# The four operand sums of a fast matrix product, moved from VectorE to GpSimd

## Chip, core and metric

The kernel runs on one core of one Trainium2 chip. The metric is the device time of one execution in microseconds. Its engines are TensorE (PE in the profile; PEld is its weight load), VectorE (DVE), ScalarE (ACT), GpSimd (POOL) and SyncE (SP, which issues most of the DMAs).

## What is computed

Retention (attention with a decay instead of a softmax) over 4 batches, 8 heads, 576 tokens and head size 64, and behind it two feed-forward layers of 2304 tokens, 512 features and 2048 hidden features, all in float32:

```python
scores = scale * np.matmul(q, k.transpose(0, 1, 3, 2))
ret = scores * Dmat[None, :, :, :]            # gamma_h ** (i - j) for i >= j, else 0
x = np.matmul(ret, v)                         # -> 2304 x 512
h = x @ moe_w_in;  x = np.maximum(0.01 * h, h) @ moe_w_out
h = np.maximum(x @ moe2_w_in, 0.0);  out = (h * h) @ moe2_w_out
```

## The kernel before, in words

**Numbers.** A float32 operand of a feed-forward product is kept as two rounded halves, `hi` (a ScalarE copy that rounds) and `lo` (a VectorE subtraction of the rest), and a product is three matmuls: hi x hi, hi x lo, lo x hi.

**The first product** of a layer is done by a Strassen-like scheme: data and weights are cut into four blocks, and seven products of sums and differences of blocks take the place of eight. The tokens are cut into three parts of 768 (`p` = 0 to 2), and the 2048 hidden features into four groups (`g`). For each layer, group and part, `first` does the seven products into the PSUM tiles `a` and `b`, in the order 0 to 6, and `second` multiplies the result by the output weights into PSUM tiles `yps`, in two halves of tokens (t = 0, 1). The sums over groups are kept in `ysb[p]`: for the first group ScalarE copies them (line 428), for later ones VectorE adds them (line 430).

**The operands of the data** are made once for each layer and part, by the generator `operands(layer, p)`: six builds in all. Of the blocks b11, b21, b12, b22 of `ysb[p]` it makes b11, b21, t2 = b22 - (b12 - b11), b22 - b12, b12 - b11, b21 - t2 and b22, in place, with the four subtractions of lines 270, 272, 275 and 281, each 128 x 768 elements. For each of the seven it writes a `hi` (line 256, ScalarE) and a `lo` (line 260, VectorE) into an `x` tile. These tiles are stored to DRAM (line 237) and loaded again for the later groups (line 304).

**When.** The builds are written out between other work by hand-set tables and a pace: `operands(0, 0)` runs in steps during the attention part (the first 87 us or so), and `operands(layer, p + 1)` during the second product of part p of group 0; `operands(1, 0)` during that of the last part of the last group of layer 0. In the same places stand the steps of the weights (`steps_in`, lines 149 to 187, and `steps_out`, lines 199 to 216), which unpack, sum and split the weights on ScalarE and VectorE. Each engine then works its own list in the order in which it was written. So one VectorE list holds the builds, the weights' steps, the sums `t` of the first product (lines 370, 384, 389), its activation (line 329), its `glo` (line 356), the output sums (line 430), and in the attention part the masked scores (line 515).

**GpSimd** has, before, only the decays of the attention part: line 524 scales q, line 528 scales k, in place, one pair for each chunk of tokens; there are 20 chunks (0 to 19), the last of each five half as long.

Waits that matter below: line 370 adds the second product (in `b`) and the ScalarE copy `s` of the first, and the fourth product can't be written into `b` before it has read; the seventh, into `a`, waits in the same way for line 384; and a `yps` group of the second half of tokens waits until the bank of the first half is read (line 428 or 430).

Of the kernel before, what the change touches and what calls it, by code (L numbers as in the profile page):

```python
# [50 lines left out]
def retention_ffn_kernel(ctx: ExitStack, tc: tile.TileContext, full, rows, half, halfv, w1, w2, const, mask, gk, out):  # L51
# [12 lines left out]
    nc = tc.nc  # L64
    sub, mul, add, mx = ALU.subtract, ALU.mult, ALU.add, ALU.max
# [23 lines left out]
    def f32(ap):  # L89
        return ap.bitcast(F32)  # L90
# [151 lines left out]
    def operands(layer, p):  # L242

        x = ysb[p].rearrange("p (k t n) -> p k t n", k=NK, t=2)
        b11, b21, b12, b22 = (x[:, k : k + 2, t] for t in range(2) for k in (0, 2))
        t2 = stage.tile([P, 2, HT], F32, tag="t2", name="t2")

        xt = {}

        def hi(i, src):  # L250
            use = layer, 0, p, i
            while uses[loaded[0]] != use or loaded[0] == used[0] + SLOTS:
                yield True
            loaded[0] += 1
            xt[i] = xs[use] = xpool.tile([P, 2, 2, HT], F32R, tag="x", name="x")
            nc.scalar.activation(xt[i][:, 0], src, AF.Copy)

        def lo(i, src):
            t = xt[i]
            nc.vector.tensor_tensor(t[:, 1], src, f32(t[:, 0]), sub)  # L260
            kept.append(((layer, 0, p, i), t))


        yield from hi(0, b11)
        yield
        yield from hi(1, b21)
        lo(0, b11)
        yield
        lo(1, b21)
        nc.vector.tensor_tensor(b11, b12, b11, sub)  # L270
        yield
        nc.vector.tensor_tensor(t2, b22, b11, sub)
        yield
        yield from hi(2, t2)
        nc.vector.tensor_tensor(b12, b22, b12, sub)
        yield
        yield from hi(3, b12)
        lo(2, t2)
        yield
        yield from hi(4, b11)  # L280
        nc.vector.tensor_tensor(b21, b21, t2, sub)
        yield
        yield from hi(5, b21)
        lo(3, b12)
        yield
        yield from hi(6, b22)
        lo(4, b11)
        yield
        lo(5, b21)
        yield  # L290
        lo(6, b22)
        yield
# [296 lines left out]
    with tc.manual_schedule():  # L589
        with tc.tile_pool(name="att", bufs=1) as pool:  # L590
# [22 lines left out]
            for i in range(n):  # L613
# [16 lines left out]
                if a < 2 * HT <= a + t:  # L630
                    builds.append(operands(0, 0))
# [26 lines left out]
        for layer in range(2):  # L658
            for g in range(NG):
# [25 lines left out]
                for p in range(NB):  # L685
                    built = [15 * p + 8]
                    if g == 0 and p + 1 < NB:
                        builds.append(operands(layer, p + 1))
                    elif layer == 0 and g == NG - 1 and p == NB - 1:
                        builds.append(operands(1, 0))  # L690

                    def in_first(m):
                        if i == p == m == 0:
                            return
                        pace(15 * p + m + 1, max(start, limit - 3))

                    def in_second(t, j, part):

                        if t or j or part in (0.5, 1):
                            pace(15 * p + 7 + 4 * t + 2 * (j + part), limit if p == NB - 1 else max(start, limit - 3))  # L700
                        load_x()

                    gs = first(layer, g, p, in_first)
                    second(layer, g, p, gs, in_second)
                    build(99)
# [58 lines left out]
```

## Time and profile before

| | us |
|---|---|
| median of 3 runs | 840.95 |
| lowest and highest run | 840.44 and 841.79 |
| span of the profiled execution | 840.4 |
| TensorE busy | 824.5 (98%) |
| VectorE busy | 601.4 (72%), 734 instructions |
| ScalarE busy | 340.2 (40%) |
| GpSimd busy | 44.3 (5%), 36 instructions, all in the first 77 us |

The span runs from the first to the last instruction; the page gives no other time of the profiled execution. It agrees with the lowest run. An engine's list is read by its rows: start, duration, line, and in brackets the idle time before it with what ended that. The reported duration of a VectorE or GpSimd instruction begins when it is issued, so time in which it was held is in it.

### The profile page before, as it was taken

Reading aid. Unit: us, or ns where it says so; the run is one execution under the profiler, and the core shown is the slowest. Engines: PE = TensorE matmul, PEld = TensorE weight load, DVE = VectorE, ACT = ScalarE, POOL = GpSimd, SP = SyncE. Lnnn points to the kernel's source line nnn. Section 1 sums busy time; section 2 is a strip of 40 time slices with the busy share of each in tenths; the row PEclk is TensorE's granted clock in tenths of the full one; section 3 lists DMA queues with packets and bytes.
Section 4 is the critical chain, followed back from the end, with each engine's and each line's share of the span. In section 5 each row is a group of like instructions: output and inputs, shape, how many; then the busy total and the mean of one; then the engine's idle time right before and its main releaser. Section 6 shows DMA issues by size and latency. Waiting matters only on the chain.

```text
span 840.4 us, 12382 instructions
## 1 busy us (share of the span) xinstructions
PE 824.5 (98%) x5084; PEld 776.9 (92%) x5084; DVE 601.4 (72%) x734; ACT 340.2 (40%) x447; POOL 44.3 (5%) x36
## 2 busy tenths in 40 slices
PE   7999999999999999999999999999999999999998
PEld 6888899999999999999999998998998998998996
DVE  4698789657666566658668879868777778754534
ACT  1454667544523433434425365543322333321211
POOL 3755000000000000000000000000000000000000
PEclk8999999999999999999999999999999999999999
DMA  9898463967646637746823554966855655735811
GB/s 349 330 322 292 170 258 114 420 250 260 247 180 250 248 135 292 259 140 233 307 101 122 191 226 163 385 246 233 296 178 203 263 182 231 263 140 199 288 51 75
DMA packets 45688, 191.01 MB, mean 227 GB/s; under 512 B 5696, under 2 KB 6720, under 8 KB 45632
## 3 DMA queue, kind: packets, MB, share of 16 engines
q1 hardware_dynamic: 45200, 189.44, 60.7%
q8 instruction: 40, 0.66, 0.3%
q10 hardware_dynamic: 432, 0.79, 0.3%
q14 instruction: 16, 0.13, 0.0%
HBM read 152.45 MB, written 37.75 MB: 226 GB/s over the span
## 4 chain that ended last, share of the span: by engine, by line
PE 84%; DVE 9%; ACT 3%; DMA 2%; issue 2%; SPq 0%; DVEq 0%; ACTq 0%
PE yps L419 44%; PE a L318 21%; PE b L318 15%; DMA raw<-in_w 1%; DVE r L515 1%; PE ops L544 1%; ACT sf L149 1%; PE ops L541 1%; DMA ysb<-in_w 1%; DVE x L260 1%; PE scps L513 1%; DVE sf L163 1%; DVE ilo L187 1%; PE sums L550 1%; DVE sf L205 1%
## 5 line engine op out<-in xcount | busy, mean ns | idle before, releaser
L318 PE MATMUL a<-x,ihi 128*128 128x384 f32 x768 | 196.1, 336 | 2.7 <-DVE t L384 2.4
L318 PE MATMUL b<-x,ihi 128*128 128x384 f32 x576 | 146.6, 335 | 0.8 <-DVE t L370 0.8
L318 PEld LDWEIGHTS a<-x,ihi 128*128 128x128 f32 x768 | 138.5, 188 | 5.8 <-DVE t L384 4.0
L419 PE MATMUL yps<-ghi,ohi 128*128 128x384 f32 x384 | 128.6, 335 | 0.6 <-ACT ysb L428 0.6
L318 PE MATMUL a<-x,ilo 128*128 128x384 f32 x384 | 128.5, 335 | 0.0
L419 PE MATMUL yps<-ghi,olo 128*128 128x384 f32 x384 | 128.3, 334 | 0.0
L419 PE MATMUL yps<-glo,ohi 128*128 128x384 f32 x384 | 128.3, 334 | 0.0
L356 DVE TENSOR_TENSOR glo<-t,ghi 128x768 fp32r<-128x768 f32 x96 | 91.7, 955 | 46.1 <-ACT ghi L351 45.6
L430 DVE TENSOR_TENSOR ysb<-yps,ysb 128x384 f32<-128x384 f32 (+1 forms) x126 | 76.0, 610 | 62.5 <-PE yps L419 62.1
L419 PE MATMUL yps<-ohi,glo 128*128 128x512 f32 x288 | 112.3, 390 | 0.0
L419 PE MATMUL yps<-olo,ghi 128*128 128x512 f32 x288 | 112.3, 390 | 0.0
L419 PE MATMUL yps<-ohi,ghi 128*128 128x512 f32 x288 | 112.1, 389 | 0.0
L351 ACT ACTIVATE ghi<-t 128x768 fp32r<-128x768 f32 x96 | 81.1, 845 | 68.5 <-DVE t L329 55.1
L318 PEld LDWEIGHTS b<-x,ihi 128*128 128x128 f32 x576 | 103.8, 188 | 1.7 <-DVE t L370 1.1
L344 ACT ACTIVATE s<-a 128x768 f32<-128x768 f32 x47 | 38.2, 814 | 156.2 <-PE a L318 156.1
L318 PE MATMUL b<-x,ilo 128*128 128x384 f32 x288 | 96.3, 334 | 0.0
L419 PEld LDWEIGHTS yps<-ghi,ohi 128*128 128x128 f32 x384 | 72.1, 188 | 1.6 <-ACT ysb L428 0.9
L318 PEld LDWEIGHTS a<-x,ilo 128*128 128x128 f32 x384 | 72.1, 188 | 0.0
L419 PEld LDWEIGHTS yps<-glo,ohi 128*128 128x128 f32 x384 | 72.1, 188 | 0.0
L419 PEld LDWEIGHTS yps<-ghi,olo 128*128 128x128 f32 x384 | 72.1, 188 | 0.0
L419 PEld LDWEIGHTS yps<-ohi,glo 128*128 128x128 f32 x288 | 54.0, 188 | 11.3
L419 PEld LDWEIGHTS yps<-olo,ghi 128*128 128x128 f32 x288 | 54.1, 188 | 11.0
(67 smaller groups left out, 997.3 us busy)
## 6 DMA issues: line engine op xcount, KB each, us to landing
x<-x SPq DMA_DIRECT2D x168, 768.0 KB, 5.9
raw<-in_w SPq DMA_DIRECT2D x62, 512.0 KB, 5.0
kv<-in_rows SPq DMA_DIRECT2D x16, 512.0 KB, 5.8
out<-ysb SPq DMA_DIRECT2D x18, 256.0 KB, 2.0
q<-in_full SPq DMA_DIRECT2D x16, 256.0 KB, 4.5
kt<-in_full SPq DMA_DIRECT2D x13, 256.0 KB, 4.7
ysb<-in_w SPq DMA_DIRECT2D x2, 512.0 KB, 6.8
kt<-in_full ACTq DMA_DIRECT2D x3, 256.0 KB, 5.6
```

The lines of the kernel that those rows point to most:

```text
L149: nc.scalar.activation(f32(a), f32(raw[:, :, 1]), AF.Abs)
L163: nc.vector.scalar_tensor_tensor(a, high, 1 << 31, a, ALU.bitwise_and, ALU.bitwise_or)
L187: nc.vector.tensor_tensor(lo[:, a:z], sf[:, a + 1 : z + 1], f32(hi[:, a:z]), sub)
L205: nc.vector.scalar_tensor_tensor(rest, high, 23, low, ALU.logical_shift_left, ALU.bitwise_or)
L260: nc.vector.tensor_tensor(t[:, 1], src, f32(t[:, 0]), sub)
L318: nc.tensor.matmul(ps[:, u, :HT], a[:, w, s], x[:, b, k], start=(start and k == 0 and i == 0), stop=(k == 1 and i == 2), skip_group_check= ...
L344: nc.scalar.activation(t, ps[:, :, :HT], AF.Copy)
L351: nc.scalar.activation(h, t, AF.Copy)
L356: nc.vector.tensor_tensor(l, t, f32(gs[key][0]), sub)
L419: nc.tensor.matmul(acc, a, b, start=(j == u == i == 0), stop=(j == 1 and u == NU - 1 and i == 2))
L430: nc.vector.tensor_tensor(y, acc, y, add)
L513: nc.tensor.matmul(ps[:n, j, p, :n], k[s, c], q[s, c], start=True, stop=True)
```

## The change

The four subtractions are issued on GpSimd; the operands, the places where they are written, and everything else stay.

```diff
@@ -267,18 +267,18 @@
         lo(0, b11)
         yield
         lo(1, b21)
-        nc.vector.tensor_tensor(b11, b12, b11, sub)
-        yield
-        nc.vector.tensor_tensor(t2, b22, b11, sub)
+        nc.gpsimd.tensor_tensor(b11, b12, b11, sub)
+        yield
+        nc.gpsimd.tensor_tensor(t2, b22, b11, sub)
         yield
         yield from hi(2, t2)
-        nc.vector.tensor_tensor(b12, b22, b12, sub)
+        nc.gpsimd.tensor_tensor(b12, b22, b12, sub)
         yield
         yield from hi(3, b12)
         lo(2, t2)
         yield
         yield from hi(4, b11)
-        nc.vector.tensor_tensor(b21, b21, t2, sub)
+        nc.gpsimd.tensor_tensor(b21, b21, t2, sub)
         yield
         yield from hi(5, b21)
         lo(3, b12)
```

GpSimd's list in the attention part, `operands(0, 0)` (`ysb_66` is `ysb[0]`, `t_557` its `t2`):

```order
+L270 TENSOR_TENSOR ysb_66<-ysb_66 128x2x384
 L528 TENSOR_TENSOR kv<-kv,gk 128x512
 L524 TENSOR_TENSOR q<-q,gq_77 128x512
 L528 TENSOR_TENSOR kv<-kv,gk 128x512
+L272 TENSOR_TENSOR t_557<-ysb_66 128x768
 L524 TENSOR_TENSOR q<-q,gq_78 128x512
 L528 TENSOR_TENSOR kv<-kv,gk 128x512
 L524 TENSOR_TENSOR q<-q,gq_79 128x512
 L528 TENSOR_TENSOR kv<-kv,gk 128x512
+L275 TENSOR_TENSOR ysb_66<-ysb_66 128x2x384
 L524 TENSOR_TENSOR q<-q,gq_80 128x256
+L281 TENSOR_TENSOR ysb_66<-ysb_66,t_557 128x2x384
```

The four subtractions stand between the decays of chunks 14 to 19; the other twenty follow on GpSimd behind the last decay, with nothing between them.

VectorE's list in the second product of layer 0, group 0, part 0, where `operands(0, 1)` is built (`ysb_67` is `ysb[1]`, `t_1164` its `t2`, `sf` and `raw` belong to the weights' steps):

```order
 L260 TENSOR_TENSOR x<-ysb_67,x 128x768
-L270 TENSOR_TENSOR ysb_67<-ysb_67 128x2x384
-L161 TENSOR_SCALAR sf<-sf 128x1024
-L163 SCALAR_TENSOR_TENSOR sf<-raw,sf 128x1024
-L272 TENSOR_TENSOR t_1164<-ysb_67 128x768
-L165 TENSOR_SCALAR sf<-sf 128x1024
-L168 SCALAR_TENSOR_TENSOR sf<-raw,sf 128x1024
-L275 TENSOR_TENSOR ysb_67<-ysb_67 128x2x384
+L161 TENSOR_SCALAR sf<-sf 128x1024
+L163 SCALAR_TENSOR_TENSOR sf<-raw,sf 128x1024
+L165 TENSOR_SCALAR sf<-sf 128x1024
+L168 SCALAR_TENSOR_TENSOR sf<-raw,sf 128x1024
```

The weights' steps close up; only the subtractions left the list.

VectorE's list in the second product of the last group and part of layer 0, where `operands(1, 0)` is built and the output sums of `ysb[2]` (`ysb_68`) are VectorE's:

```order
 L260 TENSOR_TENSOR x<-ysb_66,x 128x768
-L270 TENSOR_TENSOR ysb_66<-ysb_66 128x2x384
-L187 TENSOR_TENSOR ilo<-sf,ihi 128x1024
-L430 TENSOR_TENSOR ysb_68<-yps,ysb_68 128x384
-L272 TENSOR_TENSOR t_4206<-ysb_66 128x768
-L430 TENSOR_TENSOR ysb_68<-yps,ysb_68 128x384 x2
-L275 TENSOR_TENSOR ysb_66<-ysb_66 128x2x384
+L187 TENSOR_TENSOR ilo<-sf,ihi 128x1024
+L430 TENSOR_TENSOR ysb_68<-yps,ysb_68 128x384 x3
 L260 TENSOR_TENSOR x<-t_4206,x 128x768
```

The second to fourth output sums of the first half of tokens now follow each other behind line 187.

The waits of the moved instructions on GpSimd: line 270 waits for the `lo` of b11 (line 260, the first of a build) and, in the first build, its `hi`; line 272 for line 270; line 275 for nothing further; line 281 for the `lo` of b21 (the second) and for line 272. ScalarE's `hi` of t2, b12 and b21 wait for lines 272, 275 and 281.

## Rows read from the trace of the kernel before

**Rows 1.** The page, part 4: the chain that ended last, by engine.

```profile
PE 84%; DVE 9%; ACT 3%; DMA 2%; issue 2%; SPq 0%; DVEq 0%; ACTq 0%
```

**Rows 2.** Busy time by stretch: window, length, busy us and (instructions) of each engine.

```profile
104.00:124.00 20.00, 20.00 (x118) 19.94 (x117) 18.29 (x23) 11.87 (x20) 0.00 (x0) 1.00 0.61 236
449.00:457.00 8.00, 7.98 (x46) 7.39 (x44) 7.62 (x11) 3.26 (x5) 0.00 (x0) 1.00 0.48 197
515.00:533.00 18.00, 18.00 (x90) 15.95 (x89) 17.20 (x20) 10.92 (x16) 0.00 (x0) 1.00 0.70 268
```

**Rows 3.** Waits: who for whom, us in total, times, longest us.

```profile
PE a L318 <- DVE t L384: 2.4, 3, 1.1
...
PEld yps L419 <- DVE ysb L430: 0.6, 2, 0.3
```

**Rows 4.** VectorE's groups by line and form: xcount, busy us, mean ns.

```profile
L275 DVE TENSOR_TENSOR ysb<-ysb 128x768 f32<-128x768 f32 x6 | 5.7, 948 | 0.0
```

**Rows 5.** Timeline of GpSimd, 37 to 45 us: start, duration, instruction.

```profile
37.46 1.04 POOL L528 TENSOR_TENSOR kv<-kv,gk 128x512 f32<-128x512 f32 x1
38.47 1.26 POOL L524 TENSOR_TENSOR q<-q,gq 128x512 f32<-128x512 f32 x1
...
41.14 0.73 POOL L524 TENSOR_TENSOR q<-q,gq 128x256 f32<-128x256 f32 x1
```

**Rows 6.** Timeline of all engines, 65 to 78 us, in the attention part.

```profile
68.01 1.21 DVE L515 TENSOR_TENSOR r<-scps,mask 128x1024 f32<-128x1024 f32 x1
...
68.95 1.26 POOL L524 TENSOR_TENSOR q<-q,gq 128x512 f32<-128x512 f32 x1
...
69.15 2.15 DVE L209 SCALAR_TENSOR_TENSOR sf<-raw,sf 128x1024 uint32<-128x1024 uint32 x1
...
70.19 2.02 POOL L528 TENSOR_TENSOR kv<-kv,gk 128x512 f32<-128x512 f32 x1
...
71.23 1.79 DVE L272 TENSOR_TENSOR t<-ysb 128x768 f32<-128x768 f32 x1
...
73.21 1.13 PE L544 MATMUL ops<-q,state 128*128 128x128 f32 x8 [1.36 <-ACT state L556]
...
77.61 0.69 PE L550 MATMUL sums<-kv 128*64 128x64 f32 x16
```

**Rows 7.** Timeline of VectorE and TensorE, 104 to 123 us, build 2.

```profile
104.78 0.95 DVE L260 TENSOR_TENSOR x<-ysb,x 128x768 fp32r<-128x768 f32 x1
...
106.41 0.69 DVE L159 TENSOR_SCALAR sf<-sf 128x1024 f32<-128x1024 f32 x1 [0.67 <-ACT sf L149]
...
115.96 3.56 DVE L260 TENSOR_TENSOR x<-ysb,x 128x768 fp32r<-128x768 f32 x4
...
121.48 0.95 DVE L370 TENSOR_TENSOR t<-b,s 128x768 f32<-128x768 f32 x1
...
122.58 0.53 PE L318 MATMUL b<-x,ihi 128*128 128x384 f32 x2
```

**Rows 8.** Timeline of VectorE: line 370 of the part after builds 3 and 5.

```profile
153.99 0.96 DVE L370 TENSOR_TENSOR t<-b,s 128x768 f32<-128x768 f32 x1 [2.98 <-PE b L318]
...
498.69 0.96 DVE L370 TENSOR_TENSOR t<-b,s 128x768 f32<-128x768 f32 x1 [3.44 <-PE b L318]
```

**Rows 9.** Timeline of VectorE and TensorE, 449 to 458 us, build 4.

```profile
450.79 0.96 DVE L187 TENSOR_TENSOR ilo<-sf,ihi 128x768 fp32r<-128x768 f32 x1 [0.38 <-ACT ihi L185]
...
455.00 0.55 DVE L430 TENSOR_TENSOR ysb<-yps,ysb 128x384 f32<-128x384 f32 x1
...
455.61 0.19 PEld L419 LDWEIGHTS yps<-ghi,ohi 128*128 128x128 f32 x1 [0.27 <-DVE ysb L430]
```

**Rows 10.** Timeline of VectorE and TensorE, 515 to 533 us, build 6.

```profile
516.47 0.95 DVE L260 TENSOR_TENSOR x<-ysb,x 128x768 fp32r<-128x768 f32 x1
...
531.14 0.96 DVE L370 TENSOR_TENSOR t<-b,s 128x768 f32<-128x768 f32 x1
...
532.95 0.51 PE L318 MATMUL b<-x,ihi 128*128 128x384 f32 x2
```

## The prediction

> **What bounds the kernel now.** I read the chain of waits first. By engine it gives PE 84% and DVE 9% [rows 1], so the span is TensorE's, and VectorE matters only where the chain passes through it. The busy time by stretch shows where that can be [rows 2]: in three stretches that hold builds of the first product's operands, VectorE is busy 18.29 of 20, 7.62 of 8 and 17.20 of 18 us; a fourth lies in the attention part. The list of waits then shows what TensorE waits for: 2.4 us for `t` of line 384, and its weight loads 0.6 us for the `ysb` sums of line 430 [rows 3]. So the margins between VectorE and TensorE are small in these stretches, and what the change does to VectorE there decides; in the rest of the run VectorE has slack and the moved lines don't occur.
>
> **What it removes.** There are 24 instructions: lines 270, 272, 275 and 281, six of each. One takes 0.95 us on VectorE [rows 4]; in a row of such instructions the starts lie 0.87 us apart (four in 3.56 us) [rows 7], so a build sheds 4 x 0.87 = 3.5 us of VectorE.
>
> **What it adds.** GpSimd has no such instruction before. Its nearest rows are products of two SBUF tiles [rows 5]: line 524 takes 0.73 us for 256 elements and 1.26 us for 512, that is 0.53 us for each 256, so 1.79 us for 768. Line 528, whose second input is repeated over 64 elements, takes 1.04 us for 512, which scaled by 1.5 gives 1.56 us; 1.26 x 1.5 gives 1.89 us. I take 1.79, since line 524 has, like the moved lines, two full inputs, and keep 1.56 and 1.89 for the range. The Trainium skill, GPSIMD Engine Reference, section 3.1, states 4497 ns for such an addition of 2048 elements; an estimate scaled to 768 is 1.69 us. By that the sum below would be some 1.3 us less; no run here shows that size.
>
> The larger cost is that GpSimd's instructions do not run beside VectorE's. In [rows 6] GpSimd's line 524 runs from 68.95 to 70.21. VectorE's line 209, issued at 69.15, ends at 71.30, 1.09 us after GpSimd's end. GpSimd's line 528, issued at 70.19, ends 0.91 us after that (72.21), and VectorE's line 272, issued at 71.23, 0.81 us after that (73.02). So the two take turns, one whole instruction at a time, and each turn is 0.13 us shorter than the instruction alone. Line 515, which reads PSUM, doesn't take part: it still runs (68.01 to 69.22) when line 524 starts at 68.95, and line 524 takes the 1.26 us that it takes elsewhere [rows 5, 6]. A moved instruction therefore takes 1.79 - 0.13 = 1.66 us out of VectorE's time, where it took 0.87, unless VectorE is idle or on a PSUM sum at that moment: **0.8 us more for each, 3.2 us for a build in a full stretch.**
>
> **Build by build.** On GpSimd line 270 waits for the first `lo` (line 260) alone, 272 for 270, 275 for nothing, and 281 for the second `lo` and 272. So they can run sooner than VectorE's order had them.
>
> Build 1 (attention, 56 to 81 us) moves four instructions into GpSimd's queue between the decays of lines 524 and 528. Behind line 270 and 272 wait the decays of chunks 15 to 19, and behind those TensorE's outputs. The tightest that both push is the one of line 528 that ends at 72.21 and is read by line 550 at 77.61 [rows 6]: 5.4 us of slack against two instructions of 1.79, 3.6 us. So the decays cost nothing, or up to 1 us if turns stretch them. What counts is line 209 on VectorE: it ends at 71.30, and only then do ScalarE's next steps and line 544 (73.21, after 1.36 us of waiting for the state) follow [rows 6]. Ahead of it line 270 goes away, but both 270 and 272 now take turns with VectorE there; 272 stood behind it before. If PSUM sums and idle time covered both, that is -0.9; if neither, 2 x 1.66 - 0.87 = +2.5. Parts of each fall beside line 515. I take **+0.9**.
>
> Build 2 (104 to 120 us). VectorE ends the first `lo` at 105.73 and is then idle for 0.67 us; line 159 starts at 106.41 [rows 7]. Line 270 takes 105.85 to 107.6 on GpSimd, so line 159 is held for 1.05 us more than it had. After that VectorE had no gap up to line 370, which ends at 122.43. It sheds 3.48 us and gives three turns of 1.66: 1.05 - 3.48 + 4.98 = +2.5 us for line 370. The fourth product's matmuls into `b` start at 122.58 and need line 370; the slack is 0.15 us. After it ScalarE and VectorE are chained to line 370 as far as the seventh product, where TensorE already waits. **+2.4.** The products' operands come in time: the third `lo` by some 118, against 120.5 for the third product, one product before the fourth.
>
> Build 3 (137 to 149 us). VectorE is idle for 2.98 us before the next line 370 [rows 8]. The build costs 3.2; the rest goes to the end: **+0.3**.
>
> Build 4 (449 to 465 us) is the one with the output sums on VectorE, too. The first `lo` ends at 450.4, where VectorE's 0.38 us of idle time before line 187 begin [rows 9]; then GpSimd has 450.5 to 452.3. Line 187, ready at 450.79, waits until then. In turns follow 187 (0.87), 272 (1.66, with a sum of line 430 beside it), the second `lo` (0.87), 275 (1.66), the second 187 (1.1) and the second sum of line 430 (0.5): 452.3 + 6.66 = 458.96. Before, this sum ended at 455.55, and TensorE's next group, which needs its PSUM bank, began at 455.61 [rows 9]. That is +3.4, less the 0.3 us wait for the third sum, which it swallows: **+3.1.** Three moved instructions now stand ahead of that sum in turns, where one stood in VectorE's order.
>
> Build 5 (484 to 494 us). VectorE is idle for 3.44 us before line 370 at 498.69 [rows 8], more than 3.2: **0**.
>
> Build 6 (516 to 533 us). From the first `lo`, ended at 517.42, to line 370 at 531.14 VectorE has no gap but 0.3 us [rows 10]. 4 x 1.66 - 3.48 - 0.3 = +2.9 for line 370, which ends at 532.10; the fourth product starts at 532.95, a slack of 0.85: **+2.1**.
>
> **The sum** is 0.9 + 2.4 + 0.3 + 3.1 + 0 + 2.1 = 8.8 us. TensorE has no gap after 560 us in which to make it up. On the profiled span it is 840.4 + 8.8 = 849.2; the median of the runs is 840.95, 0.5 above the span, and gives **849.7 us**. With 1.56 us for a moved instruction builds 1, 2, 4 and 6 lose 2, 4, 3 and 4 times 0.23, and build 3 its 0.3: 5.5, so 846.4. With 1.89 and builds 3 and 5 out of slack by 0.6 each, 11.3 or 852.3.
>
> **Rivals.**
> Faster: GpSimd's instructions run beside VectorE's at 0.95 us. Then only what TensorE waits for VectorE comes back: 0.9 at line 544, 1.1 (the longest of the three) at line 384 in build 2 [rows 3], 0.3 in build 4, 0.1 elsewhere, 2.4 in all: 838.5. It decides from the point where a VectorE instruction with two SBUF inputs keeps its length under a GpSimd instruction; [rows 6] show two that don't. The Trainium skill, Perfetto Trace Analysis, section Optimizing Scalar/DVE Operations, says that with a saturated VectorE moving work to GpSimd may make sense, and warns in the same place that the shared port may spoil it; the rows bear out the warning. I give 0.06.
>
> No change: the turns fall where VectorE reads PSUM or waits for ScalarE, as in builds 3 and 5, in builds 2, 4 and 6 too. Only build 1 is left, 841 to 842. Against it speak the stretches in [rows 2]; for it, that ScalarE's copies also move and can fall better. 0.10.
>
> Slower still: GpSimd's chain becomes the bound. If it got only each second turn, or 2.5 us for an instruction, the third `lo` would come after the third product wants it (2.2 us of margin in build 2, about the same in build 6), and the decays of build 1 would be late: 3 us more in build 1 and some 1 in 2 and 6 each, 854.5. For it speaks that line 528 took 2.02 us in turns; against it, that this is mostly waiting. 0.14.
>
> That the move doesn't happen is out: the 24 instructions stand on GpSimd in the changed program's order.
>
> **How the numbers follow.** The forecast has 0.70. What a measurement tells from no change is 0.2%, 1.7 us. The forecast and the slower rival give slower 0.84; no change has 0.10, faster 0.06. The range leaves out the two rivals on the fast side and the far end of the slow one: from 843.5, where one of the three terms of 2 to 3 us is missing and the short duration holds, to 853.5.
>
> **What would show it.** GpSimd's busy time rises by at least 24 x 1.79 = 43 us; lines 270 to 281 take 1.7 to 2.9 us each. The forms of VectorE with two SBUF inputs (lines 187, 216, 260, 163) get longer in the mean, and lines 430 and 515 don't. TensorE's waits for line 370 grow to 4 us or more in sum, and those of its weight loads for line 430 from 0.6 to 3 or more. The blocks around builds 2, 4 and 6 get longer, and those between, without moved instructions, keep their length. It is wrong if VectorE's instructions keep their length beside GpSimd's, or if line 370 of build 2 comes no later after the product before it.

## The result and the profile after

The changed kernel takes **853.23 us** (median of four runs, 851.47 to 854.63), the kernel before 841.04 us beside it (840.44 to 841.79): a ratio of 1.0143, interval 1.013 to 1.0155, or 12.2 us more. The forecast was 849.7, with a range from 843.5 to 853.5. The profile after is of the run of 851.47 us; its span is 849.7 us. Below, three executions that took far longer than the rest (906 to 4656 us, two of them of the kernel before) are in the medians and not in the ratios.

The page's first and fourth part of the profile after (busy us, share of the span, instructions; then the chain that ended last, by engine):

```profile
PE 824.9 (97%) x5084; PEld 777.0 (91%) x5084; DVE 609.9 (72%) x710; ACT 339.4 (40%) x447; POOL 99.7 (12%) x60
...
PE 77%; DVE 11%; DMA 5%; ACT 3%; issue 3%; SPq 0%; ACTq 0%; DVEq 0%
```

VectorE runs 24 instructions fewer than before (710 against 734) and is still busy 8.5 us longer (609.9 against 601.4). That is the change in one line: it took work from VectorE and gave it none of the time back. TensorE's share of the chain fell from 84% [rows 1] to 77%, and that of the DMAs rose from 2% to 5%.

The moved instructions are the four groups of 128x768 among GpSimd's groups by line and form (xcount, busy us, mean ns):

```profile
L281 POOL TENSOR_TENSOR ysb<-ysb,t 128x768 f32<-128x768 f32 x6 | 14.4, 2397 | 0.0
L275 POOL TENSOR_TENSOR ysb<-ysb 128x768 f32<-128x768 f32 x6 | 14.3, 2383 | 0.0
L272 POOL TENSOR_TENSOR t<-ysb 128x768 f32<-128x768 f32 x6 | 13.9, 2320 | 0.4
L270 POOL TENSOR_TENSOR ysb<-ysb 128x768 f32<-128x768 f32 x6 | 12.5, 2076 | 408.1 <-DVE x L260 408.1
```

Waits of TensorE after (us in total, times, longest), which answer to [rows 3]:

```profile
PE b L318 <- DVE t L370: 3.5, 3, 2.3
PE a L318 <- DVE t L384: 3.4, 4, 1.8
PE yps L419 <- DVE ysb L430: 3.3, 1, 3.3
```

Line 430 now holds TensorE up for 3.3 us at once, where the list of before had 0.6 us of weight loads. Line 384 went from 2.4 to 3.4 us, and line 370, with 3.5 us now, had 0.8 before.

Where the 12.2 us arise is read from the starts of the same TensorE products in the two timelines. The offset (after minus before) stays nearly constant between the builds and steps at them:

| Place | before, us | after, us | offset | step |
|---|---|---|---|---|
| attention, ahead of build 1 (L513) | 57.19 | 54.37 | -2.82 | |
| build 1 (L513) | 69.66 | 67.82 | -1.84 | +1.0 |
| build 2, fourth product | 122.58 | 123.23 | +0.65 | +2.5 |
| build 2, seventh product | 130.68 | 132.10 | +1.42 | +0.8 |
| after build 3 | 181.97 | 183.03 | +1.06 | -0.4 |
| after build 4 | 463.31 | 470.22 | +6.91 | +5.85 |
| after build 5 | 508.11 | 515.02 | +6.91 | 0 |
| build 6, to its end | 539.30 | 548.57 | +9.27 | +2.4 (three steps) |

The first offset is no gain of the change. In the profile before, TensorE's granted clock was 0.55 from 17 to 24 us, in the one after 1.00, and the profiles of the experiments differ there in the same way, whatever the builds do. From build 1 on the steps add up to 12.1 us, as the medians do.

The largest step, build 4, in the timelines of VectorE and GpSimd after (start, duration, instruction), with TensorE's three matmuls in question; it answers to [rows 9]:

```profile
451.84 2.35 DVE L187 TENSOR_TENSOR ilo<-sf,ihi 128x768 fp32r<-128x768 f32 x1 [0.38 <-ACT ihi L185]
454.12 0.54 DVE L430 TENSOR_TENSOR ysb<-yps,ysb 128x384 f32<-128x384 f32 x1
454.59 2.13 DVE L260 TENSOR_TENSOR x<-ysb,x 128x768 fp32r<-128x768 f32 x1
456.64 2.82 DVE L187 TENSOR_TENSOR ilo<-sf,ihi 128x1024 fp32r<-128x1024 f32 x1
459.39 1.47 DVE L430 TENSOR_TENSOR ysb<-yps,ysb 128x384 f32<-128x384 f32 x3
```

```profile
451.54 1.84 POOL L270 TENSOR_TENSOR ysb<-ysb 128x768 f32<-128x768 f32 x1 [301.55 <-DVE x L260]
453.46 2.45 POOL L272 TENSOR_TENSOR t<-ysb 128x768 f32<-128x768 f32 x1
455.86 2.52 POOL L275 TENSOR_TENSOR ysb<-ysb 128x768 f32<-128x768 f32 x1
458.34 2.81 POOL L281 TENSOR_TENSOR ysb<-ysb,t 128x768 f32<-128x768 f32 x1
```

```profile
456.38 0.34 PE L419 MATMUL yps<-ghi,olo 128*128 128x384 f32 x1
459.98 0.69 PE L419 MATMUL yps<-ghi,ohi 128*128 128x384 f32 x1 [3.27 <-DVE ysb L430]
460.47 0.52 PE L419 MATMUL yps<-glo,ohi 128*128 128x384 f32 x1
```

Read the ends, not the starts. Line 270 ends at 453.38, line 187 at 454.19; 272 at 455.91, line 260 at 456.72; 275 at 458.38, the second 187 at 459.46; 281 at 461.15. The engines alternate, instruction for instruction. GpSimd's 272, 275 and 281 end 1.72, 1.66 and 1.69 us after the VectorE instruction ahead of them. Only line 430, which reads PSUM, keeps its 0.54 us, though it lies wholly inside line 272. The three sums behind the second 187 come late, and TensorE stands for 3.27 us.

Then there is a second thing, which the prediction had not: the matmuls behind that wait take 0.52 us in place of 0.33. Busy time by stretch of the profile after (window, length, busy us of PE, PEld, DVE, ACT, POOL, then the granted clock, DMA share and GB/s):

```profile
459.00:461.00 2.00, 1.02 (x3) 1.02 (x4) 2.00 (x5) 0.99 (x2) 2.00 (x1) 0.58 0.25 98
461.00:466.00 5.00, 5.00 (x17) 5.00 (x17) 1.83 (x2) 1.58 (x2) 0.15 (x1) 0.50 0.66 270
```

The granted clock there is the lower of its two levels, 1.2 GHz; before it was 1.00 in this stretch, with 31 matmuls in the five microseconds instead of 17. Of the 5.85 us of build 4, 3.3 are the wait and some 2.6 the clock.

### The profile page after: what moved, and what is told of

Same layout as the page of the kernel before. It is cut to its first block, busy times and chain, and to the rows that moved or that the text cites. A ratio compares the mean times of both kernels' runs of the same rounds, so it can differ in the third digit from the quotient of the medians.

```text
span 849.7 us, 12387 instructions
## 1 busy us (share of the span) xinstructions
PE 824.9 (97%) x5084; PEld 777.0 (91%) x5084; DVE 609.9 (72%) x710; ACT 339.4 (40%) x447; POOL 99.7 (12%) x60
## 4 chain that ended last, share of the span: by engine, by line
PE 77%; DVE 11%; DMA 5%; ACT 3%; issue 3%; SPq 0%; ACTq 0%; DVEq 0%
PE yps L419 41%; PE a L318 20%; PE b L318 14%; DVE x L260 2%; DMA kt<-in_full 1%; DVE ilo L187 1%; DMA raw<-in_w 1%; DMA x<-x 1%; DVE r L515 1%; DMA gq<-in_const 1%; ACT sf L149 1%; DVE sf L209 1%; DMA kv<-in_rows 1%; DVE sf L205 1%; DVE t L370 1%
## 5 line engine op out<-in xcount | busy, mean ns | idle before, releaser
L419 PEld LDWEIGHTS yps<-ohi,ghi 128*128 128x128 f32 x288 | 54.1, 188 | 12.5 <-ACT ysb L428 1.5
```

Of the source, the lines that this page charges most:

```text
L419: nc.tensor.matmul(acc, a, b, start=(j == u == i == 0), stop=(j == 1 and u == NU - 1 and i == 2))
```

## Experiments

Line numbers of the experiments are shifted by the lines that they add; each text says which line of the kernel before is meant where it matters. Each had runs of the kernel before beside it, with medians from 840.73 to 841.16 us; a ratio is against those.

**The builds apart.** Each moves lines 270, 272, 275 and 281 as the change does, but only in some builds (line numbers here and in the next are higher by one).

```diff
+        on = nc.gpsimd if (layer, p) == (1, 0) else nc.vector
-        nc.vector.tensor_tensor(b11, b12, b11, sub)
+        on.tensor_tensor(b11, b12, b11, sub)
...
```

Build 4 alone:

> Only the build at 450 us, operands(1, 0), makes its four sums and differences on GpSimd; the other five builds make them on VectorE as before. Theory A (turns, and then the clock): in the profile after, TensorE stood 3.3 us for line 430 behind this build, and then ran 6.8 us at half the granted clock, which it did not in the profile before; the two together moved the stretch behind it by 5.85 us. So this kernel should take about 841.0 + 5.8 = 846.9 us, with the half clock somewhere in 450 to 465 us. Theory B (turns alone; the half clock is a matter of the run, as the one at the start of the profile before was): 841.0 + 3.1 = 844.1 us, with a wait of some 3 us for line 430 and the full clock behind it. Theory C (GpSimd's instructions are only longer and cover hides them; what was lost was lost elsewhere): within 1 us of 841.

All but build 4 (the condition turned round):

> All builds but operands(1, 0) make their four sums and differences on GpSimd; the one at 450 us makes them on VectorE as before. By the offsets between the two profiles the attention's build gave +1.0, the second +3.2, the third -0.3, the sixth +2.2, the fifth nothing. Theory A: 841.0 + 6.1 = 847.1 us, and no stretch of half clock in 450 to 465 us. Theory B (the half clock is not bound to the wait for line 430 and takes its 2.6 us in any case): 849 to 850 us. The sum of this kernel's loss and that of the one with operands(1, 0) alone should be the whole change's 12.2 us if the builds do not act on each other.

Builds 3 and 5 alone:

> Only the builds operands(0, 2) and operands(1, 1), behind the second products of the first and the fourth piece, make their sums and differences on GpSimd, eight instructions out of 24. The prediction gave the third build 0.3 us and the fifth nothing, since VectorE had 10 us and more of idle time behind them; the offsets after say -0.3 and 0. If cover decides: 841.0 within 0.5 us, with lines 270 to 281 at 1.7 to 2.4 us each all the same. If the price goes by the count of moved instructions (12.2 us for 24, 0.5 us each): 845.

| Moved | us (median) | ratio, interval |
|---|---|---|
| build 4 | 844.96 | 1.0051 [1.0036, 1.0066] |
| all but 4 | 848.06 | 1.0084 [1.0062, 1.0105] |
| 3 and 5 | 840.81 | 0.9999 [0.9987, 1.0011] |

4.2 and 7.3 us make 11.5 of the 12.2: in the medians the builds add up, though they divide otherwise than the steps of the one profile (5.85 and 6.2). Builds 3 and 5 cost nothing, though their instructions take 2174 to 2564 ns in the mean there, so the price does not go by the count. It goes by whether VectorE has idle time behind.

In build 4 alone the profile repeats wait and clock:

```profile
453.00:457.00 4.00, 0.73 (x4) 0.53 (x3) 4.00 (x5) 1.85 (x3) 4.00 (x2) 0.79 0.48 197
457.00:460.00 3.00, 3.00 (x11) 3.00 (x10) 2.32 (x3) 1.58 (x2) 0.63 (x1) 0.50 0.24 100
```

The offset rises by 5.6 us there. The median is only 4.2 us up; not every run need have lost as much to the clock. Mean clocks of single runs were 0.992 to 0.998, never 1.000 in ten runs, where the kernel before had 1.000 in 19 of its 74 runs beside the experiments. With all but build 4 moved, the stretch 449 to 465 us has the full clock throughout. But this profile shows the lower clock in two other places: behind build 2's wait of 2.3 us, and in the attention from 73.9 to 77.2 us (0.50), around the end of a wait of 2.2 us at line 545 (544 of before):

```profile
128.00:131.00 3.00, 3.00 (x13) 3.00 (x12) 0.96 (x2) 3.00 (x5) 0.00 (x0) 0.58 1.00 297
...
74.06 2.05 PE L545 MATMUL ops<-q,state 128*128 128x128 f32 x8 [2.21 <-ACT state L557]
```

In the profile of the change itself the clock stayed at 1.00 behind the same wait of build 2. Counted over the fourteen traces of this case, from 25 us on: all ten stands of TensorE of 3.27 us and more came with the lower clock, six of the nine between 2.12 and 2.69 us did, and none of those of 0.8 to 2.0 us.

**Half of the instructions.** Lines 275 and 281 alone, in all builds.

> In all six builds lines 275 and 281 run on GpSimd, lines 270 and 272 stay on VectorE: half of the moved instructions in every place. If each moved instruction takes its turn in VectorE's row (0.8 us each where VectorE is full): half of the 9.6 us that the builds cost without the half clock, 841.0 + 4.8 = 845.8 us, and 848.4 if TensorE's pause at 460 us is still long enough to bring the half clock. If GpSimd's chain of four is what TensorE waits for (each of the four waiting for the one before), two of four leave it time: 841 to 843.

Measured: 845.61 us, ratio 1.0057 [1.004, 1.0074], +4.9 us: half. TensorE's wait for line 430 in build 4 fell from 3.27 to 1.19 us, and the clock there was full:

```profile
456.58 0.44 PE L420 MATMUL yps<-ghi,ohi 128*128 128x384 f32 x1 [1.19 <-DVE ysb L431]
```

In this profile the offset also fell by 1.4 us at 74 us, in the attention, which looked like a gain. So these two lines were moved in build 1 alone:

> Only in the attention's build, operands(0, 0), lines 275 and 281 run on GpSimd, two instructions in all. In the profile with lines 275 and 281 moved in all builds the offset fell by 1.4 us at 74 us where the whole change gained nothing: line 209 ran alone there (1.21 us against 2.15 before), so ScalarE's copy behind it was done earlier and the copies of the state did not stand behind that, and TensorE's wait of 1.36 us at line 544 was gone. If that comes from the two instructions: 841.0 - 1.1 = 839.9 us, faster than both kernels. If it is the luck of who asks first in that run: 841.0 within 0.4 us.

840.58 us, ratio 0.9994 [0.9982, 1.0006]. The offset did fall by 1.4 us at 74 us again, but it had risen by 1.0 at 57 us. The gain is not there.

**GpSimd's work without its results.** Is it VectorE held, or ScalarE and TensorE waiting for GpSimd's results? Here VectorE keeps everything, and GpSimd does 20 subtractions of the same size whose result nobody uses.

```diff
         nc.vector.tensor_tensor(b11, b12, b11, sub)
+        if scr is not None:
+            nc.gpsimd.tensor_tensor(scr, f32(xt[0][:, 0]), f32(xt[0][:, 1]), sub)
...
```

> All sums and differences stay on VectorE as before; beside each of those of the second to sixth build GpSimd gets a subtraction of the same size whose result nobody uses (20 instructions more, which read the first or second operand tile). So GpSimd's work of the change is there, and no wait for its results. If the turns with VectorE are the price (VectorE's instructions held while GpSimd's run): in the three full stretches four times some 1.7 us each against no relief on VectorE, so 5 to 7 us a build in the second, fourth and sixth, some 1 to 3 us in the third and fifth, 857 to 865 us in all, and TensorE's waits for lines 370 and 430 grow as in the changed kernel. If the price was the wait for GpSimd's longer instructions (the chain 270, 272, 281 and ScalarE behind it): 841.0 within 0.5 us.

Measured: 867.40 us, ratio 1.0317 [1.03, 1.0334], +26.6 us. Nobody waits for these results, so GpSimd's work costs by itself, without any wait for what it makes. That such waits are not what TensorE stands for in the change is read from its own profile: the stands that it adds there end with VectorE's lines 370, 384, 430 and 515 and, once, with ScalarE's line 428 (build 6, below). The size was more than expected, and the wait of TensorE that is largest in sum had an unexpected name (line 353 is line 344 of before, ScalarE's copy `s`; 428 and 439 are 419 and 430):

```profile
PE a L327 <- ACT s L353: 14.2, 5, 5.4
...
PE yps L428 <- DVE ysb L439: 5.8, 1, 5.8
```

The result had been put into the buffers of just that copy, so the run was repeated with a buffer of its own.

> The kernel with subtractions beside took 867.4 us, above the 857 to 865 expected, and its trace shows why the figure can't be read as it stands: the unused result lay in the buffer pair of ScalarE's copies `s`, and TensorE waited 14.2 us for line 353's copy, which it never does in the kernel before. Here the same 20 subtractions on GpSimd read the same tiles, but write one small buffer of their own (8-bit elements, a buffer that nothing else uses). Turns alone: 853 to 862 us, no wait of TensorE for ScalarE's copy `s`, VectorE's lines 187 and 261 with longest times of 2.3 to 2.8 us. If what was lost there was the buffer: 841 to 843 us.

Measured: 868.06 us, ratio 1.031 [1.0288, 1.0333]; the wait for the copy is 14.2 us as before. The buffer was not the cause. ScalarE works in order, and ahead of the copy stood its `x` copies, which waited 41.4 us in sum (up to 10.6 at a time) for the `t` that VectorE now made late. Both expectations were too low. They priced the turns on TensorE's waits for VectorE, and neither what stands behind a late VectorE in ScalarE's queue nor the clock: in the first of the two profiles it was 0.50 from 123 to 129, from 468 to 474 and from 553 to 559 us, around stands of 5.45, 5.75 and 3.69 us. How the excess divides between the two is not shown. Line 260 (261 there) takes 1190 ns in the mean against 974 before, as in the change (1270).

**GpSimd's work without reading.** The same places, with fills in place of subtractions.

```diff
+            nc.gpsimd.tensor_copy(scr[:, 0, :1], f32(xt[0][:, 1, 0, :1]))
+            nc.gpsimd.memset(scr, 0.0)
+            nc.gpsimd.memset(scr, 0.0)
...
```

> As the kernel before, with work beside it on GpSimd that reads nothing: at each of the four places of the second to sixth build a copy of 128x1 that sets the time, and two fills of 128x768 with zeros, whose result nobody uses. Turns between instructions that read: GpSimd busy some 40 instructions more, the two-input instructions of VectorE (lines 260, 187, 357) as long as before, 841 to 842.5 us. Turns between any instructions of the two engines: as the kernel with subtractions beside, some 10 us and more. If GpSimd being awake at all (its instruction stream, its semaphores) costs: in between, by the number of its instructions.

Measured: 840.71 us, ratio 1.001 [0.9997, 1.0022]; no cost. GpSimd and VectorE in build 4 of this kernel:

```profile
452.25 0.80 POOL L279 COPY scr<-x 128x1 f32<-128x1 f32 x1
453.11 0.74 POOL L280 MEMSET scr<- 128x768 f32 x1
```

```profile
452.06 0.95 DVE L261 TENSOR_TENSOR x<-ysb,x 128x768 fp32r<-128x768 f32 x1
452.93 0.95 DVE L271 TENSOR_TENSOR ysb<-ysb 128x768 f32<-128x768 f32 x1
```

The fill at 453.11 lies inside line 271 (270 of before), and both take their usual time. The copy of one element per partition, which reads, takes 0.80 us where another of the same form, at 450.40, while VectorE was idle, took 0.18: it ends at 453.05, when VectorE's line 261 has ended at 453.01. So beside VectorE's instructions with two SBUF inputs it is the reading on GpSimd that takes turns, whatever its size.

By the Trainium skill (SBUF - State Buffer, Who interferes with whom), only a port pair that the two engines share causes contention, as an exclusive lock held by a whole instruction; GpSimd work that only writes does not contend with a two-input VectorE instruction. These traces agree: 0.74 us and 0.95 us side by side for the fill, 0.80 for the copy.

A fill is not free beside every instruction, though. Four of the 40 took 1.17 to 1.25 us, all beside single-input instructions of 1024 elements, which take turns with it. In build 2:

```profile
106.05 0.98 DVE L159 TENSOR_SCALAR sf<-sf 128x1024 f32<-128x1024 f32 x1 [0.68 <-ACT sf L149]
```

```profile
106.54 1.17 POOL L275 MEMSET scr<- 128x768 f32 x1
```

Line 159, 0.69 us alone [rows 7], waits for the fill that ends at 106.48, and the next fill waits for line 159, which ends at 107.03. The time of this kernel does not show them.

**The clock.** Build 4 alone on GpSimd once more, with 14 matmuls whose result nobody uses ahead of TensorE's wait.

```diff
+                    if (layer, g, p, t, j, e) == (0, NG - 1, NB - 1, 1, 0, 1):
+                        fill = wide(1, "fill")
+                        for _ in range(14):
+                            nc.tensor.matmul(fill[:, 0, :HT], gs[key][0][:, 0, :P], gs[key][0][:, 1], start=True, stop=True)
```

> As the kernel in which only operands(1, 0) is on GpSimd (844.96 us), with 14 matmuls of 128x384 whose result nobody uses put before TensorE's place of the 3.3 us wait (ahead of the 55th matmul of the second products there, some 2.4 us of work into a free bank), so that TensorE stands for under 1 us. If the half clock behind that place is the answer to TensorE's standing still: full clock in 450 to 465 us, the stretch up to 463 us longer by 3.1 us and not by 5.6, and a median 1 to 2.6 us below 844.96. If it is a matter of the run: half the clock again, 845 us.

TensorE's timeline, and the stretch behind (lines 424 and 435 are 419 and 430 of before):

```profile
453.93 2.59 PE L415 MATMUL fill<-ghi 128*128 128x384 f32 x14
...
457.41 0.44 PE L424 MATMUL yps<-ghi,ohi 128*128 128x384 f32 x1 [0.89 <-DVE ysb L435]
```

```profile
457.00:460.00 3.00, 2.59 (x15) 2.59 (x16) 3.00 (x5) 1.80 (x3) 1.58 (x1) 1.00 0.00 0
460.00:464.00 4.00, 4.00 (x25) 4.00 (x24) 2.37 (x5) 0.20 (x1) 0.00 (x0) 1.00 0.97 393
```

TensorE stands for 0.89 us and the clock stays at 1.00. The median is 843.64 us, ratio 1.0031 [1.0019, 1.0043], 1.3 us below the kernel without the fill, and two of its runs had a mean clock of 1.000. The profile supports that the drop answers to the stand; the medians point the same way, though their intervals overlap.

**Shorter turns.** Are the turns whole instructions? Build 4 alone on GpSimd, each moved instruction cut into two.

```diff
+                for k in range(2):
+                    nc.gpsimd.tensor_tensor(o[:, k], a[:, k], b[:, k], sub)
```

> Only the build operands(1, 0) is on GpSimd, as in the kernel that took 844.96 us, but each of its four instructions is cut into two of 128x384: eight instructions, the same elements. If the unit of a turn is the whole instruction, a VectorE instruction is held for some 0.9 us instead of 1.7 us at a time, so line 187, line 260 and the second line 187 ahead of the second sum of line 430 lose 3 x 0.8 us less: TensorE stands about 1 us there instead of 3.3, the clock stays, and the median is 842 to 842.5 us. If GpSimd's work as a whole must be done first (its length is what counts, in however many pieces): 845 to 846 us.

Measured: 840.70 us, ratio 0.9989 [0.9975, 1.0004]. The price of build 4 is gone, where the expectation left 1 to 1.5 us of it. VectorE in that stretch (lines 267 and 437 are 260 and 430 of before):

```profile
452.48 1.30 DVE L267 TENSOR_TENSOR x<-ysb,x 128x768 fp32r<-128x768 f32 x1
453.70 2.03 DVE L187 TENSOR_TENSOR ilo<-sf,ihi 128x1024 fp32r<-128x1024 f32 x1
455.66 1.47 DVE L437 TENSOR_TENSOR ysb<-yps,ysb 128x384 f32<-128x384 f32 x3
```

The second line 187 is held to 2.03 us instead of 2.82, line 260 to 1.30 instead of 2.13. TensorE's wait is 0.85 us and the clock stays. The elements that GpSimd processes are the same; what changed is the length of one hold, and the number of instructions.

The same for all builds, in halves and in quarters (128x192):

> The changed kernel (853.2 us) with each of the 24 moved instructions cut into two of 128x384. With turns of whole instructions: the holds in front of line 430 in build 4 and in front of line 370 in builds 2 and 6 are half as long each, but where VectorE has no gap it then meets more of them; build 4 some 1 us, builds 2 and 6 between half and all of their 3.2 and 2.2 us, build 1 about 1: 845 to 848.5 us. If only GpSimd's total length counts, or its chain of waits: 853 us and more.

> The changed kernel with each moved instruction cut into four of 128x192 (96 instructions on GpSimd); whole it took 853.2 us, in halves 847.1, so +12.2 and +6.0. If a hold of VectorE costs by its length and its instructions are held at most once each, the price halves once more: some +3, 844 us, with lines 187 and 163 at most 0.6 us longer than alone. If a part of the +6.0 is the chain of 270, 272 and 281 on GpSimd and the copies behind it (TensorE waited 4.4 us for line 351's copies in the halves), which gets longer with each cut (a 384 piece took 0.9 us and more, not half of 1.84): 847 to 849 us.

| Pieces for each moved instruction | us (median) | ratio, interval |
|---|---|---|
| 1 (the change) | 853.23 | 1.0143 [1.013, 1.0155] |
| 2 | 847.12 | 1.0077 [1.0054, 1.01] |
| 4 | 858.35 | 1.0191 [1.0171, 1.0211] |

Halves cost half, as expected; quarters cost more than the whole, where 844 or 847 to 849 us was expected. TensorE's waits for ScalarE's copy `s` (351 and 352 are line 344 of before; halves first) and busy time of build 2's stretch in quarters:

```profile
PE a L325 <- ACT s L351: 4.4, 4, 2.0
```

```profile
PE a L326 <- ACT s L352: 11.9, 4, 4.2
...
104.00:124.00 20.00, 17.93 (x104) 17.61 (x102) 13.77 (x14) 9.57 (x16) 15.15 (x16) 1.00 0.48 196
```

In the halves three of ScalarE's waits for GpSimd's results in build 2 (2.65, 2.52 and 2.07 us) stand ahead of that `s`. In quarters VectorE is busy for 13.77 of the 20 us, against 18.29 before [rows 2]; it is no longer the bound. GpSimd gets one turn between two VectorE instructions, so its four instructions, now sixteen, take 15.15 us, and ScalarE waits for their results: for `t` up to 5.8 us. That is the rival in which GpSimd's chain becomes the bound, in a kernel where it holds. None of these versions is measurably faster than the kernel before.

## Why the prediction was right, and where its sizes were off

**Turns of whole instructions** were the mechanism, and the runs isolate it: reading GpSimd work alone costs (867), work of the same places that only writes does not (840.7), and shorter pieces shorten the holds. The rival that GpSimd runs beside VectorE is out. A turn was put at 1.66 us and measured 1.66 to 1.72; a moved instruction alone was put at 1.79 and takes 1.84 (line 270 above).

**The range** held the time by 0.3 us, and that part is luck. Its upper end came from longer instructions and from a part of the slower rival; what filled it is the clock behind build 4 and a late load behind build 2, and the prediction has neither. The time lies nearer to the slower rival's 854.5 than to the forecast, but not by that rival's mechanism: TensorE's third products don't wait for a late `lo`, and its matmuls wait for GpSimd as little as before (0.4 us, at line 550).

**The builds**, predicted and measured in us: 1: 0.9, 1.0. 2: 2.4, 3.3. 3: 0.3, -0.4. 4: 3.1, 5.85. 5: 0, 0. 6: 2.1, 2.4. The sum was 8.8 and is 12.1.

- *Build 4* is the term that was mis-sized. Its wait was right: TensorE's next group came 3.3 us later, as worked out from four turns. What was missing is the 2.6 us of lower clock behind it. The prediction followed who waits for whom, and took TensorE's speed after the wait for granted.
- *Build 2*: the fourth product came 2.5 us later, as predicted. The step that failed is the one behind it, that nothing more is lost as far as the seventh product, where TensorE waits anyway. It waits longer there: 1.83 us where the longest was 1.1 [rows 3]. The timeline of TensorE after at these two products:

```profile
123.23 0.61 PE L318 MATMUL b<-x,ihi 128*128 128x384 f32 x2 [2.33 <-DVE t L370]
132.10 0.61 PE L318 MATMUL a<-x,ihi 128*128 128x384 f32 x2 [1.83 <-DVE t L384]
```

What came late there is a load of weights. SyncE issues it behind stores that wait for VectorE's line 260, so it goes out 0.95 us later than before, and it takes 7.6 us to land in place of 7.0. ScalarE's line 149 needs these weights, VectorE's line 203 needs line 149, and line 384 stands behind line 203. SyncE and ScalarE before; SyncE, ScalarE and VectorE after:

```profile
119.37 2.49 SPq L132 DMA_DIRECT2D raw<-in_w  x2
127.73 1.14 ACT L149 ACTIVATE sf<-raw 128x1024 f32<-128x1024 f32 x1 [0.61 <-DVE ilo L187]
```

```profile
120.32 2.49 SPq L132 DMA_DIRECT2D raw<-in_w  x2
129.28 1.17 ACT L149 ACTIVATE sf<-raw 128x1024 f32<-128x1024 f32 x1 [1.42 <-DVE glo L356]
130.49 0.69 DVE L203 TENSOR_SCALAR sf<-sf 128x1024 f32<-128x1024 f32 x1 [0.52 <-ACT sf L149]
```

The profile puts line 149's wait down to line 356, but that one only ends at the same moment: before, line 149 began while line 356 ran. Line 149 starts 1.55 us later than before, line 203 and the seventh product 1.4 us, where the fourth product was 0.65 us later. So it is not a backlog on VectorE, which stands idle for 0.52 us ahead of line 203, but a load that VectorE's delay held back. Why the load takes 0.6 us longer to land is not shown.

- *Build 1* had the right size at the wrong place. The wait at line 544 did not grow (1.28 us, 1.36 before [rows 6]). What came late was line 515, behind a line 207 that was held, and TensorE waited for it at line 513. VectorE's and TensorE's timelines after:

```profile
65.11 1.53 DVE L207 TENSOR_SCALAR sf<-sf 128x1024 uint32<-128x1024 uint32 x1
66.56 1.21 DVE L515 TENSOR_TENSOR r<-scps,mask 128x1024 f32<-128x1024 f32 x1
```

```profile
67.82 1.16 PE L513 MATMUL scps<-q,kt 64*128 64x128 f32 x16 [0.91 <-DVE r L515]
```

In the profile with all builds but build 4 moved it is the place that was predicted: TensorE waits 2.21 us for the state at line 544 (545 there, above), 0.85 more than before. So where this build costs is not the same in the two profiles.

- *Build 6* went as predicted up to the fourth product. Against the offset ahead of the build, line 370 ended 2.7 us later, where 2.9 was predicted, and the product came 1.9 us later; the rest came up to the seventh product. Ahead of it lies a wait of TensorE that the prediction does not have, for ScalarE's output copy of line 428. That copy stood behind a line 149 that waited 3.33 us for VectorE's line 216, held to 2.75 us. It is no more than a part of the 1.9, since line 370 decides when the fourth product starts. The wait, and the fourth product, after:

```profile
529.42 0.50 PE L419 MATMUL yps<-ohi,ghi 128*128 128x512 f32 x1 [1.10 <-ACT ysb L428]
541.75 0.62 PE L318 MATMUL b<-x,ihi 128*128 128x384 f32 x2 [0.33 <-DVE t L370]
```

- *The signs named ahead*: GpSimd's busy time rose from 44.3 to 99.7 us, by 55.4 (at least 43 was asked). VectorE's lines 260 and 187 got longer in the mean (974 to 1270 ns; the 1024 form of 187 from 1216 to 1391), and the median of line 430 stayed at 557. TensorE's weight loads waited 3.6 us for line 430 (3 or more was asked). Line 370's waits came to 3.5 us where 4 were asked; line 384's grew by 1.0 beside them.

What stays open: why the lower clock comes with some stands of 2.1 to 2.7 us and not with others, and how the 6 us of the halves divide between holds of VectorE and waits for GpSimd.

## What to carry to other kernels

Before work is moved from VectorE to GpSimd, look in the trace at a VectorE instruction with SBUF inputs that overlaps a GpSimd one: if its end moves behind GpSimd's, price a moved instruction at GpSimd's length in VectorE's own row, and expect the cost only where VectorE has no idle time behind it. The length of a hold can be cut by cutting the instruction, as far as GpSimd, which gets one turn for each of VectorE's, still delivers in time. Follow, too, what a late VectorE holds back in other queues: here ScalarE's copies behind line 216, and a load of weights behind SyncE's stores. And price a stand of TensorE with the clock behind it: here 3.3 us of waiting cost 5.85.

## What the runs showed of the hardware that was not expected

- VectorE instructions with a single SBUF input are held too, those that run at 0.69 us for 1024 elements [rows 7]. In build 2 after, lines 159 and 161 took 1.80 and 2.33 us:

```profile
104.55 1.80 DVE L159 TENSOR_SCALAR sf<-sf 128x1024 f32<-128x1024 f32 x1 [0.67 <-ACT sf L149]
...
108.80 2.33 DVE L161 TENSOR_SCALAR sf<-sf 128x1024 uint32<-128x1024 uint32 x1
```

- The turns alternate strictly while both engines have work: no engine got two turns in a row in build 4. A GpSimd copy of a single element per partition waits for the VectorE instruction ahead of it too (0.80 us against 0.18). A fill, which reads nothing, takes no turns with VectorE's two-input instructions, and does with its single-input ones of 1024 elements (1.17 us against 0.74).
- TensorE's granted clock went to its lower level with a stand of 3.3 us and stayed there through 461 to 466 us, though TensorE was busy for the whole of these five microseconds.
